# A fused attention, expert and mixer kernel: the front of the mixer reordered

## The chip, the cores and the metric

The kernel runs on one core of a Trainium2 chip. The metric is the device time of one execution, in microseconds. Before the change the median of three runs is 624.88 us (624.0 to 626.03). TensorE multiplies matrices, VectorE, ScalarE and GpSimd work on vectors, SyncE (SP) only starts transfers. In the rows they are PE (PEld for its weight loads), DVE, ACT, POOL and SP.

## The reference

Three layers follow each other, on 2 batches of 768 tokens with 384 values each. The first is a linear attention with a delta rule. The second sends every token to one of 8 experts. The third, the mixer, is the one that the change is mostly about:

```
def _moe2_ref(x, w_ch1, w_ch2):
    X = np.fft.fft(x, axis=1)
    X = np.fft.fft(X, axis=2)
    mixed = np.real(X).astype(np.float32)
    u = x + mixed
    mu = np.mean(u, axis=-1, keepdims=True)
    var = np.mean((u - mu) ** 2, axis=-1, keepdims=True)
    un = (u - mu) / np.sqrt(var + 1e-06)
    ch = np.maximum(un @ w_ch1, 0.0) @ w_ch2
    return (u + ch).astype(np.float32)
```

`w_ch1` is 384 x 1536, `w_ch2` 1536 x 384. In the expert layer each token's chosen expert is the argmax of its gate logits, or the expert of the token before it where a local gate says so; its output is p[e] * (relu(x @ w1[e]) @ w2[e]).

## The kernel before

**Splits.** To keep float32 accuracy, every operand of a large product is split into a high part (rounded, by a ScalarE copy) and a low part (the difference, by VectorE or GpSimd). A product then takes three matmuls: high by high, low by high, high by low. For the weights these are `whi` (ScalarE) and `wlo` (VectorE, which then also issues the load of the weights six steps ahead on SP).

**Routing and experts.** `route` ranks the tokens of each expert on VectorE and TensorE and makes the lists for gathers and scatters. `moe_main` runs 32 steps of one quarter expert each: `h` (first product, relu and split), `whi` and `wlo` for later steps, `o` (second product). It starts with `chosen`, the low splits of three weight blocks, and the transposes of expert 0's tokens (`xtr`). Between the steps it decodes the mixer's weights, which arrive as 64-bit numbers (`decoding`, a generator that is advanced step by step). The last step ends with two scatters of token rows to `x2d` in HBM, issued by GpSimd. Behind them stand 24 warm-up products (`WARMM`) and the splits of the last three weight blocks, 35 to 37.

**The mixer** reads `x2d` again. The sequence of 768 is treated as 6 x 128. `load` brings x of one batch in three transfers (pairs of row blocks, i = 1, 2, 0), then `ur`, the same rows in output order, on SP; two of its six tiles are gathered by GpSimd. `sums` (even half) and `difs` (odd half) combine the blocks; `split` splits the results (`zh`, `zl`). `along` does one residue k2: products along the sequence (`yp`), their split (`evac`), products along the features (`fp`), then the two output tiles m that mirror each other, each added to its tile of `ur` (`add`). `stats` takes mean and variance and normalises (`un`), `untr` transposes and splits the result (`uT`). `mlp1` and `mlp2` then run over 12 tiles in `GROUPS=(2,4,4,2)`; the tiles of a batch come in the order 2, 4, 1, 5, 0, 3, so group 0 is the two tiles of k2 = 2 of the first batch. `warm` runs products on the first part of x to keep TensorE busy.

**The order of the work** in the mixer is not written out. Each step is a generator that yields costs (engine, ns), flags to wait for and resources to take or return. `Order` simulates them once, when the program is built, and emits instructions in the order in which its engines would grant them. Priorities are in `MP` (lower goes first), `EB` holds a bias for VectorE in the choice between VectorE and GpSimd (`tt`, `eng`); it is a bias on the planned cost. What comes out is a fixed order on each engine; every engine works in order.

Of the kernel before, what the change touches and what calls it, by code (L numbers as in the profile page):

```python
# [6 lines left out]
F32 = mybir.dt.float32  # L7
# [722 lines left out]
class Rest:  # L730
# [4 lines left out]
    def route(s,keep,pool,ps,lg):  # L735
# [54 lines left out]
        s.Wr=T("W",[128,4,2,12,8],F16); s.ph=T("ph",[128,4,2,12],F16); pp=s.pp=pool.tile([128,4,12],F16,name="pp")  # L790
# [8 lines left out]
        V.tensor_copy(out=pp[:,0],in_=tok)  # L799
        s.parts(0)  # L800
# [139 lines left out]
    def moe_main(s):  # L940
        dec=s.decoding(); s.sc=[]; s.scattered=[]; last=None
        s.chosen()
        s.wlo(0); s.wlo(1)
        for k in range(3): s.xtr(0,k,"h",3)
        s.wlo(2)
        next(dec)
        for q in range(32):
# [6 lines left out]
            last=x  # L954
            s.wlo(q+3)
# [19 lines left out]
    WARMM=24  # L975
# [102 lines left out]
    def load(s,b):  # L1078
# [27 lines left out]
    def tt(s,out,a,b,op,x):  # L1106
        e,c=s.eng(469,956,s.EB.get(x,0))
        yield c
        e.tensor_tensor(out=out,in0=a,in1=b,op=op)  # L1109
    def stt(s,out,a,x,b):  # L1110
        yield ("V",469)
        s.nc.vector.scalar_tensor_tensor(out=out,in0=a,scalar=x,in1=b,op0=ALU.mult,op1=ALU.add)
    def buf(s,n,b): return s.fq.tile([128,384],F32,tag=n,name=n,bufs=1)
    def sums(s,b):
# [53 lines left out]
    def split(s,b,k,z):  # L1168
        yield ("+","z")
        h=s.fq.tile([128,384],F32R,tag="zh",name="zh",bufs=4); l=s.fq.tile([128,384],F32R,tag="zl",name="zl",bufs=4)  # L1170
        yield ("A",413)
# [6 lines left out]
    EB={'q1': -500, 'q0': 0, 'D1': -2000, 'z0': -500, 'S0': -2000, 'S1': 1000, 'z1': 1000, 'D0': 500}  # L1178
    WARM,PHASE=18,0
    MP={'M1': 0, 'M2': 2.48, 'R': 0, 'F': 0.26, 'a02': 1.67, 'a01': 2.48, 'a00': 0, 'a03': 0.58, 'a12': 1.4, 'a11': 0.19, 'a10': 2.06, 'a13': 1.84, 'L1': 1.44, 'u11': 2.35, 'q00': 1.26, 'z02r': 1.07, 'z11r': 1.2, 'e10': 0.65, 'D1': 1.9, 'q01': 2.35, 'u14': 0.69, 'q03': 0.52, 'q11': 1.03, 'e12': 2.33, 'S1': 0.4, 'z02i': 1.72, 'D0': 1.75, 'u13': 0.39, 'q02': 1.0, 'q05': 2.0, 'z01i': 0.51, 'u00': 0.67, 'u02': 0.79, 'e02': 1.68, 'z12r': 0.29, 'q14': 2.09, 'e01': 2.48, 'e11': 2.42, 'e00': 1.31, 'q15': 2.4, 'u03': 1.82, 'u15': 1.94, 'e03': 1.49, 'u10': 1.32, 'z12i': 1.87, 'z11i': 1.57, 'z01r': 1.37, 'u12': 2.13, 'u01': 1.05, 'e13': 1.85, 'q13': 0.71, 'q04': 2.47, 'q12': 0.26, 'q10': 0.16, 'u05': 1.84, 'S0': 0.76, 'u04': 1.14}  # L1180
    def along(s,b,k2):

        nc,o=s.nc,s.o; V=nc.vector
        ks=[("0",0)] if k2==0 else [("3",3)] if k2==3 else [(f"{k2}r",k2),(f"{k2}i",3+k2)]
        for n,_ in ks: yield f"z{b}{n}"
        yield ("+","Y")
        Y=[s.fq.tile([128,3,256],F32R,tag=f"Y{i}",name="Y",bufs=2) for i in range(2)]
        for d in range(3):
            yield ("+","h")
            p=s.ps.tile([128,256],F32,tag="h",name="yp",bufs=3)  # L1190
            yield ("T",330*len(ks),0) if d<2 else ("T",330*len(ks))
            n=0
            for z,t in ks:
                for a,c in ((0,0),(1,0),(0,1)):
                    nc.tensor.matmul(out=p,lhsT=s.z[b,z][a][:,128*d:128*d+128],rhs=s.seq[c][t],start=(n==0),stop=(n==3*len(ks)-1)); n+=1  # L1195
            s.add_(f"e{b}{k2}",s.evac(b,k2,d,p,Y,330*len(ks)))
# [4 lines left out]
        for d in range(3):  # L1201
            yield f"Y{b}{k2}{d}"
            yield ("T",620)
            for x in range(2):
                for a,c in ((0,0),(1,0),(0,1)):
# [4 lines left out]
        yield ("A",213)  # L1210
# [3 lines left out]
        for k,o1,o2 in kk:  # L1214
            yield ("+","m")
            m=s.fq.tile([128,384],F32,tag="m",name="m",bufs=1)
            yield ("V",540)
# [6 lines left out]
        for k in ks: yield f"u{b}{k}"  # L1224
        yield from s.stats(b,ks)
    def evac(s,b,k2,d,p,Y,t):
        yield ("",t+200)
        yield ("A",264)
        s.nc.scalar.activation(out=Y[0][:,d],in_=p,func=AF.Copy)
        yield ("V",335)  # L1230
# [8 lines left out]
    def stats(s,b,ks):  # L1239
        nc,o=s.nc,s.o; V=nc.vector; n=len(ks)  # L1240
        yield ("+","st")
        T=lambda nm,sh: s.fp.tile([128]+sh,F32,tag=nm,name=nm,bufs=2)
        ag=T("ag",[2,2]); v=T("vs",[4,2])
        for i,k in enumerate(ks):
            st=T(f"bs{i}",[6])
            yield ("V",469)
            V.bn_stats(out=st,in_=s.ur[b][:,k])
            yield ("V",75)
            V.bn_aggr(out=ag[:,i],in_=st)
        m,va=ag[:,0:n,0],ag[:,0:n,1]  # L1250
        v0,sd,r,nm=[v[:,i,0:n] for i in range(4)]
        yield ("V",75)
        V.tensor_scalar(out=v0,in0=va,scalar1=1e-6,scalar2=None,op0=ALU.add)
        yield ("A",95)
        nc.scalar.activation(out=sd,in_=v0,func=AF.Sqrt)
        yield ("V",80)
        V.reciprocal(out=r,in_=sd)
        yield ("V",75)
        V.tensor_tensor(out=r,in0=r,in1=v0,op=ALU.mult)
        yield ("V",75)  # L1260
        V.tensor_tensor(out=r,in0=r,in1=sd,op=ALU.add)
        yield ("V",75)
        V.tensor_scalar(out=r,in0=r,scalar1=0.5,scalar2=None,op0=ALU.mult)
        yield ("V",80)
        V.reciprocal(out=r,in_=r)
# [38 lines left out]
    def warm(s):  # L1304
# [9 lines left out]
        if s.WARM: yield from s.left_xa(0)  # L1314
    def w_ch1(s,x,k,f): return s.W[32+f//2][:,x,f%2,128*k:128*k+128]
# [167 lines left out]
```

## Time and profile before

The profiled execution took 627.96 us, its span is 626.2 us, with a mean granted TensorE clock of 0.905.

| engine | busy us | share of the span | instructions |
|---|---|---|---|
| PE (matmul) | 507.9 | 81% | 4986 |
| DVE | 421.7 | 67% | 950 |
| ACT | 323.7 | 52% | 745 |
| POOL | 88.1 | 14% | 89 |

Attention fills the span up to about 250 us, routing follows until 269 us, the experts until 410 us, and the mixer runs from there to the end. The shares are means over these stages, so they tell little of one stage; the rows below are of single stretches. In a row of the timeline, times are us from the span's start, then the busy time, the engine, the line of the kernel, the operation, what is written and read, the count, and in brackets the idle time before it with what ended it. In a row of the chain of waits stand the start, the length and the work that the end waited for. Two clock levels occur: 1.00 is 2.4 GHz, 0.50 is 1.2 GHz.

### The profile page before, as it was taken

How to read it: one execution, taken by the hardware profiler on the slowest of the kernel's cores; microseconds unless marked ns; L12 is line 12 of the kernel's file. 1: busy time of each engine (PE TensorE's matmuls, PEld its weight loads, DVE VectorE, ACT ScalarE, POOL GpSimd, SP SyncE). 2: the span in 40 equal slices, each digit the busy share in tenths (PEclk: the TensorE clock that was granted, in tenths of full speed). 3: DMA queues.
4: the chain of work that ended last, by engine and by line, in shares of the span. 5: the costliest groups of instructions: out<-in, count | busy, mean ns of one | idle time of the engine just before them, and what ended most of it. 6: DMA issues, size and time to landing. Idle time of an engine off the chain costs nothing.

```text
span 626.2 us, 12592 instructions
## 1 busy us (share of the span) xinstructions
PE 507.9 (81%) x4986; PEld 482.3 (77%) x4986; DVE 421.7 (67%) x950; ACT 323.7 (52%) x745; POOL 88.1 (14%) x89
## 2 busy tenths in 40 slices
PE   0333047894888999599999999978899999999997
PEld 0233037784778898589999999977799998998997
DVE  7968997868997963687788788767886731221122
ACT  3465177877788897346665656543454321111111
POOL 5000000000000000223212232243640000000010
PEclk9955558877989999599999999989699999999999
DMA  6722230341331525699789795235000000010010
GB/s 231 143 59 77 67 62 8 113 93 51 77 70 28 95 49 165 197 312 349 263 286 326 274 304 187 93 133 188 1 1 1 14 13 1 2 50 1 1 50 26
DMA packets 71438, 69.85 MB, mean 112 GB/s; under 512 B 44286, under 2 KB 63523, under 8 KB 71376
## 3 DMA queue, kind: packets, MB, share of 16 engines
q1 hardware_dynamic: 68240, 59.16, 31.8%
q0 software_dynamic: 3136, 9.85, 4.6%
q8 instruction: 40, 0.66, 0.4%
q14 instruction: 22, 0.18, 0.1%
HBM read 53.53 MB, written 7.86 MB: 98 GB/s over the span
## 4 chain that ended last, share of the span: by engine, by line
PE 38%; issue 13%; POOL 3%; DVE 2%; DMA 1%; ACT 1%; POOLq 0%; SPq 0%; ACTq 0%
PE mp L1330 12%; PE mop L1356 12%; PE hp L916 5%; PE op L927 4%; PE fp L1206 2%; PE yp L1195 1%; POOL xg L898 1%; POOL x2d L936 1%; PE up L1288 1%; POOL ur L1098 1%; DMA x2d<-ot,sim 1%; DMA xa<-x2d 0%; POOL e L1109 0%; POOL tab L1074 0%; PE xtp L904 0%
## 5 line engine op out<-in xcount | busy, mean ns | idle before, releaser
L1340 DVE SCALAR_TENSOR_TENSOR ml<-mp,mh 128x256 fp32r<-128x256 f32 (+1 forms) x48 | 26.8, 558 | 98.5 <-ACT mh L1338 98.3
L1330 PE MATMUL mp<-uT,ws 128*128 128x256 f32 (+1 forms) x432 | 85.3, 343 | 0.2 <-DVE ml L1340 0.2
L1338 ACT ACTIVATE mh<-mp 128x256 fp32r<-128x256 f32 (+1 forms) x48 | 23.6, 491 | 115.7 <-PE mp L1330 115.7
L1356 PE MATMUL mop<-ws,mh 128*128 128x384 f32 x288 | 81.6, 338 | 0.0
L1330 PEld LDWEIGHTS mp<-uT,ws 128*128 128x128 f32 x432 | 69.5, 193 | 9.0 <-DVE ml L1340 0.8
L916 PE MATMUL hp<-xT,ws 128*128 128x256 f32 x576 | 74.0, 283 | 1.1 <-DVE xT L907 1.1
L916 PEld LDWEIGHTS hp<-xT,ws 128*128 128x128 f32 x576 | 72.5, 190 | 1.3 <-DVE xT L907 1.3
L927 PE MATMUL op<-ws,hh 128*128 128x384 f32 x256 | 72.1, 343 | 0.0
L309 PEld LDWEIGHTS <-KT 128*128 128x128 f16 x576 | 25.9, 113 | 58.7 <-issue 31.0
L309 PE MATMUL ga<-ST,KT 128*128 128x64 f16 x288 | 16.4, 227 | 57.0 <-DVE ST L305 50.6
L891 DVE TENSOR_TENSOR ws<-raw,ws 128x1536 fp32r<-128x1536 f32 x32 | 56.0, 1751 | 0.0
L1356 PEld LDWEIGHTS mop<-ws,mh 128*128 128x128 f32 x288 | 52.8, 188 | 0.8
L888 ACT ACTIVATE ws<-raw 128x1536 fp32r<-128x1536 f32 x32 | 47.4, 1487 | 2.6 <-DMA raw<-moe_w 2.6
L1356 PE MATMUL mop<-ws,ml 128*128 128x384 f32 x144 | 48.3, 335 | 0.0
L927 PEld LDWEIGHTS op<-ws,hh 128*128 128x128 f32 x256 | 46.8, 188 | 0.0
L927 PE MATMUL op<-ws,hl 128*128 128x384 f32 x128 | 42.9, 335 | 0.0
L919 DVE SCALAR_TENSOR_TENSOR hl<-hp,hh 128x512 fp32r<-128x512 f32 x32 | 22.1, 691 | 27.4 <-ACT hh L918 27.3
L898 POOL DMA_INDIRECT xg<-xd,gm x16 | 21.7, 1356 | 120.4 <-DMA raw<-moe_w 113.7
L918 ACT ACTIVATE hh<-hp 128x512 fp32r<-128x512 f32 x32 | 19.0, 593 | 36.0 <-PE hp L916 36.0
L936 POOL DMA_INDIRECT x2d<-ot,sim x16 | 21.5, 1347 | 101.6 <-ACT ot L932 99.2
L368 DVE TENSOR_TENSOR tmp<-Gu,P 128x31 f32<-128x31 f32 (+15 forms) x93 | 31.5, 339 | 1.9
L370 DVE TENSOR_TENSOR P<-P,tmp 128x31 f32<-128x31 f32 (+15 forms) x93 | 31.4, 337 | 1.7
(268 smaller groups left out, 1224.1 us busy)
## 6 DMA issues: line engine op xcount, KB each, us to landing
raw<-moe_w SPq DMA_DIRECT2D x64, 384.0 KB, 5.5
x<-moe_w_ch SPq DMA_DIRECT2D x24, 384.0 KB, 6.3
qp<-q SPq DMA_DIRECT2D x6, 512.0 KB, 3.9
kp<-k SPq DMA_DIRECT2D x6, 384.0 KB, 4.7
vp<-v SPq DMA_DIRECT2D x6, 384.0 KB, 5.2
xd<-yb SPq DMA_DIRECT2D x48, 48.0 KB, 1.7
xa<-x2d SPq DMA_DIRECT2D x6, 384.0 KB, 4.0
tab<-seq POOLq DMA_DIRECT2D x2, 768.0 KB, 7.2
```

Of the source, the lines that this page charges most:

```text
L309: s.nc.tensor.matmul(out=out,lhsT=st[l],rhs=mv[m],start=(first and i==0),stop=True,skip_group_check=True)
L368: nc.vector.tensor_tensor(out=x,in0=Gu[:,k,k+1:32].unsqueeze(2).to_broadcast([128,m,n]),in1=P[:,k,0:n].unsqueeze(1).to_broadcast([128,m,n] ...
L370: nc.vector.tensor_tensor(out=P[:,k+1:32,0:n],in0=P[:,k+1:32,0:n],in1=x,op=ALU.subtract)
L888: s.nc.scalar.activation(out=s.W[q][:,0].rearrange("p s c -> p (s c)"),in_=s.raw[q],func=AF.Copy)
L891: s.nc.vector.tensor_tensor(out=W[1],in0=s.raw[q],in1=W[0],op=ALU.subtract)
L898: nc.gpsimd.indirect_dma_start(out=s.xg[e][t],out_offset=None,in_=s.xd,in_offset=bass.IndirectOffsetOnAxis(ap=s.gi[:,8*t+e:8*t+e+1],axis=0))
L916: nc.tensor.matmul(out=p[:,i],lhsT=s.W[q][:,a,i,128*k:128*k+128],rhs=xT[b][:,k],start=(n==0),stop=(n==8)); n+=1
L927: nc.tensor.matmul(out=s.po[t],lhsT=hs[a][:,i,128*t:128*t+128],rhs=s.W[q][:,b,i,384:768],start=(g==0 and i==0 and n==0),stop=(g==3 and i== ...
L936: i=s.nc.gpsimd.indirect_dma_start(out=s.x2d,out_offset=bass.IndirectOffsetOnAxis(ap=s.si[:,c:c+1],axis=0),in_=ot,in_offset=None,bounds_ch ...
L1330: nc.tensor.matmul(out=p,lhsT=s.w_ch1(a,k,f),rhs=s.uT[g][b][:,k,0:N],start=(n==0),stop=(n==8)); n+=1
L1340: nc.vector.scalar_tensor_tensor(out=hl,in0=p,scalar=0.0,in1=hh,op0=ALU.max,op1=ALU.subtract)
L1356: nc.tensor.matmul(out=pm[t],lhsT=hs[a][:,128*t:128*t+128],rhs=s.w_ch2(b,f),start=(f==0 and n==0),stop=(f==11 and n==2))
```

## The change

- `route`: the token number is copied right after the one-hot of the expert is made; its product with that one-hot (`Wt`) stands behind the rank products, and one product each with the two rank halves takes the place of `parts(0)`.
- `moe_main`: the low split of weight block 1 goes behind the transposes, that of block 2 into the first step. At the end GpSimd sets a word to zero (queued behind the scatters), VectorE copies it, and only then come the low split of block 35 and the splits of 36 and 37. The warm-up is 38 products.
- `load`: `ur` is loaded once the third part of x has landed. ScalarE writes one column of it from x, which SP's transfer then waits for.
- `EB`: all sums and low splits of the first batch go to VectorE (-9000). `sums` makes the difference of parts 1 and 2, and starts its split, ahead of the third part. Planned costs and `MP` are new throughout, `WARM` is 16 instead of 18.
- `along`, first batch, k2 = 2: the products of the imaginary part run first, into all three banks, those of the real part follow, and each of the two tiles gets its own `stats`. The order of the three matmuls of a product is high-high, high-low table, low-high.
- `stats`: ScalarE takes half the standard deviation straight from the variance (scale 0.25, bias 0.25e-6), one reciprocal, two fused VectorE operations and one more reciprocal give the refined 1/sd: two VectorE operations less.
- `fill`: four 128-column products on a unit matrix at a time, with the lowest priority and a pause of 500 ns in the plan, from the imaginary part's split until group 0 is complete. They hold one of the four `o` banks.
- `mlp1`: the three kinds of matmul are the outer loop and the three blocks of k the inner one.

```diff
@@ route
+        pp=s.pp=pool.tile([128,4,12],F16,name="pp"); pp0=pp[:,0]
         V.tensor_tensor(out=Ot,in0=it,in1=b3(e),op=ALU.is_equal)
+        V.tensor_copy(out=pp0,in_=tok)
+        Wt=T("Wt",[128,12,8],F16)
...
+        V.tensor_tensor(out=Wt,in0=Ot,in1=b3(pp0),op=ALU.mult)
...
-        V.tensor_copy(out=pp[:,0],in_=tok)
-        s.parts(0)
+        for h in range(2): V.tensor_tensor(out=s.Wr[:,0,h],in0=Wt,in1=b3(s.hi[:,h]),op=ALU.mult)
@@ moe_main
-        s.wlo(0); s.wlo(1)
+        s.wlo(0)
         for k in range(3): s.xtr(0,k,"h",3)
-        s.wlo(2)
+        s.wlo(1)
...
+            if q==0: s.wlo(2)
             s.wlo(q+3)
...
+        z=s.wk.tile([128,2],F32,name="z")
+        s.nc.gpsimd.memset(z[:,0:1],0.0)
+        s.nc.vector.tensor_copy(out=z[:,1:2],in_=z[:,0:1])
+        for _ in dec: pass
         s.wlo(35)
-        for _ in dec: pass
         for q in (36,37):
             s.whi(q); s.wlo(q)
-    WARMM=24
+    WARMM=38
@@ load
+        yield f"xa{b}0"
+        yield ("A",150)
+        nc.scalar.activation(out=ur[:,0,0:1],in_=xa[0][:,0:1],func=AF.Copy)
         yield ("Q",475)
         nc.sync.dma_start(out=ur[:,0:4],in_=w[:,0:4])
-        yield f"xa{b}0"
@@ sums
         yield from s.tt(t[3],t[1],t[2],A,f"S{b}")
+        yield from s.tt(t[1],t[1],t[2],S,f"S{b}")
+        s.add_(f"z{b}2i",s.split(b,"2i",t[1]))
         yield f"xa{b}0"
         yield from s.tt(t[0],x[0],x[3],A,f"S{b}")
         yield from s.left_xa(b)
-        yield from s.tt(t[1],t[1],t[2],S,f"S{b}")
-        s.add_(f"z{b}2i",s.split(b,"2i",t[1]))
@@ class
-    EB={'q1': -500, 'q0': 0, 'D1': -2000, 'z0': -500, 'S0': -2000, 'S1': 1000, 'z1': 1000, 'D0': 500}
-    WARM,PHASE=18,0
+    EB={'q1': 500, 'q0': -9000, 'D1': 0, 'z0': -9000, 'S0': -9000, 'S1': -500, 'z1': 1000, 'D0': -9000}
+    WARM,PHASE=16,0
@@ along
+        early=b==0 and k2==2
+        def product(d,zs,first,last):
+            for z,t in zs:
+                for a,c in ((0,0),(0,1),(1,0)):
+                    nc.tensor.matmul(out=p[d],lhsT=s.z[b,z][a][:,128*d:128*d+128],rhs=s.seq[c][t],start=first,stop=last and z==zs[-1][0] and a==1); first=False
+        p={}
+        if early:
+            yield f"z{b}2i"
+            for d in range(3):
+                yield ("+","h")
+                p[d]=s.ps.tile([128,256],F32,tag="h",name="yp",bufs=3)
+                yield ("T",375,0)
+                product(d,ks[1:],True,False)
+            ks=ks[:1]
...
-        for k in ks: yield f"u{b}{k}"
-        yield from s.stats(b,ks)
+        if early:
+            for k in ks: s.add_(f"u{b}{k}",s.stats(b,[k]))
+        else: yield from s.stats(b,ks)
@@ stats
-        V.tensor_scalar(out=v0,in0=va,scalar1=1e-6,scalar2=None,op0=ALU.add)
-        nc.scalar.activation(out=sd,in_=v0,func=AF.Sqrt)
+        nc.scalar.activation(out=h,in_=va,func=AF.Sqrt,scale=0.25,bias=s.eps)
...
+        V.scalar_tensor_tensor(out=w,in0=va,scalar=1e-6,in1=r,op0=ALU.add,op1=ALU.mult)
+        V.scalar_tensor_tensor(out=w,in0=w,scalar=0.25,in1=h,op0=ALU.mult,op1=ALU.add)
@@ fill (new, called in mixer behind warm)
+        yield "z02i"
+        yield ("+","o")
+        p=s.ps.tile([128,512],F32,tag="o",name="wq",bufs=4)
+        while "n01" not in s.o.flags and s.o.now<100000:
+            yield ("T",220)
+            for _ in range(4): s.nc.tensor.matmul(out=p[:,0:128],lhsT=s.K["identh"],rhs=s.K["identh"],start=True,stop=True)
+            yield ("",s.FILL)
+        yield ("-","o")
@@ mlp1
-                for k in range(3):
-                    for a,b in ((0,0),(1,0),(0,1)):
-                        nc.tensor.matmul(out=p,lhsT=s.w_ch1(a,k,f),rhs=s.uT[g][b][:,k,0:N],start=(n==0),stop=(n==8)); n+=1
+                for a,b in ((0,0),(1,0),(0,1)):
+                    for k in range(3): nc.tensor.matmul(out=p,lhsT=s.w_ch1(a,k,f),rhs=s.uT[g][b][:,k,0:N],start=(n==0),stop=(n==8)); n+=1
```

## Rows read from the trace of the kernel before

**Rows 1.** Windows: stretch, length, busy (count) of PE, PEld, DVE, ACT, POOL, clock, DMA
```profile
435.00:438.80 3.80, 2.28 (x19) 1.94 (x17) 3.20 (x14) 1.45 (x4) 0.64 (x1) 1.00 0.02 8
438.80:444.70 5.90, 4.06 (x15) 3.11 (x16) 4.91 (x10) 3.23 (x8) 5.62 (x6) 0.50 0.01 3
444.70:449.00 4.30, 4.30 (x20) 4.30 (x21) 3.85 (x7) 0.77 (x2) 2.26 (x3) 0.50 0.00 0
449.00:480.00 31.00, 30.56 (x233) 29.16 (x233) 24.49 (x76) 15.64 (x41) 9.93 (x9) 1.00 0.00 1
```

**Rows 2.** Chain of waits: start us, us, what
```profile
409.96 2.44 POOL x2d L936
...
412.71 3.46 DMA x2d<-ot,sim
...
416.29 3.09 DMA xa<-x2d
...
444.70 2.29 PE mp L1330 x9
...
619.26 2.62 PE mop L1356 x15
```

**Rows 3.** Timeline, routing and first expert: start, us, engine, line, operation [idle before]
```profile
256.95 0.17 DVE L813 TENSOR_TENSOR ph<-pp,hi 128x24 f16<-128x24 f16 x1
...
269.13 4.57 PE L916 MATMUL hp<-xT,ws 128*128 128x256 f32 x36 [1.08 <-DVE xT L907]
```

**Rows 4.** Timeline around the scatters, VectorE and GpSimd
```profile
378.91 1.15 POOL L936 DMA_INDIRECT x2d<-ot,sim  x1 [11.36 <-ACT ot L932]
...
409.75 1.75 DVE L891 TENSOR_TENSOR ws<-dec,ws 128x1536 fp32r<-128x1536 f32 x1
...
412.12 3.43 DVE L891 TENSOR_TENSOR ws<-dec,ws 128x1536 fp32r<-128x1536 f32 x2 [0.62 <-ACT ws L888]
...
412.71 2.06 POOL L936 DMA_INDIRECT x2d<-ot,sim  x1 [0.30 <-issue]
```

**Rows 5.** Timeline, VectorE's first sums
```profile
419.40 0.56 DVE L1109 TENSOR_TENSOR d<-xa 128x384 f32<-128x384 f32 x1 [3.85 <-DMA xa<-x2d]
...
423.72 0.57 DVE L1109 TENSOR_TENSOR e<-xa 128x384 f32<-128x384 f32 x1 [1.22 <-DMA xa<-x2d]
...
424.21 0.55 DVE L1109 TENSOR_TENSOR d<-xa 128x384 f32<-128x384 f32 x1
```

**Rows 6.** Line 1094, the load of ur: both transfers, issue to landing
```profile
DMA to landing us min/median/max: 7.5/8.3/9.1
```

**Rows 7.** Chain of waits: products along the sequence and features at full clock
```profile
461.36 0.65 PE fp L1206 x6
...
472.97 1.07 PE yp L1195 x9
```

**Rows 8.** Timeline, TensorE: the first feature products
```profile
429.81 2.26 PE L1206 MATMUL fp<-tab,Y 128*128 128x194 f32 x18 [0.39 <-DVE Y L1231]
```

**Rows 9.** Statistics by tile and timeline, up to the first MLP product
```profile
L1247 DVE BATCH_NORM_STATS2 bs<-ur x12: 526/551/561, 434.8 to 501.2; 128x6 f32<-128x384 f32 x12
...
434.63 1.01 POOL L1109 TENSOR_TENSOR ur<-ur,m 128x384 f32<-128x384 f32 x1 [2.93 <-DVE m L1219]
...
441.08 0.87 PE L1288 MATMUL up<-ca,un 128*128 128x128 f32 x3 [1.26 <-ACT un L1272]
...
442.50 1.35 DVE L1109 TENSOR_TENSOR zl<-e,zh 128x384 fp32r<-128x384 f32 x1
```

**Rows 10.** Windows of lines 1195 and 1206 alone: PE, PEld, clock, DMA
```profile
419.40:444.70 25.30, 8.14 (x45) 6.75 (x45) 0.77 0.46 164
...
419.40:444.70 25.30, 4.65 (x36) 4.25 (x36) 0.77 0.46 164
```

**Rows 11.** Timeline, group 1: its last tile's split, its first product
```profile
480.15 0.55 DVE L1295 TENSOR_TENSOR uT<-up,uT 128x384 fp32r<-128x384 f32 x1
...
490.95 2.26 PE L1330 MATMUL mp<-uT,ws 128*128 128x512 f32 x9
```

More of the change, by code (lines that the diff above doesn't have):

```diff
@@ L789, in route @@
         hi=s.hi=T("hi",[128,2,12],F16); lo=T("lo",[128,12],F16)
-        s.Wr=T("W",[128,4,2,12,8],F16); s.ph=T("ph",[128,4,2,12],F16); pp=s.pp=pool.tile([128,4,12],F16,name="pp")
+        s.Wr=T("W",[128,4,2,12,8],F16); s.ph=T("ph",[128,4,2,12],F16)
         oh=s.oh=pool.tile([128,12,128],F16,name="oh")
@@ L1106, in tt @@
     def tt(s,out,a,b,op,x):
-        e,c=s.eng(469,956,s.EB.get(x,0))
+        e,c=s.eng(550,1270,s.EB.get(x,0))
         yield c
@@ L1110, in stt @@
     def stt(s,out,a,x,b):
-        yield ("V",469)
+        yield ("V",550)
         s.nc.vector.scalar_tensor_tensor(out=out,in0=a,scalar=x,in1=b,op0=ALU.mult,op1=ALU.add)
@@ L1188, in along @@
         for d in range(3):
[L1189 to L1196, printed above, removed]
+            if not early:
+                yield ("+","h")
+                p[d]=s.ps.tile([128,256],F32,tag="h",name="yp",bufs=3)
+            yield ("T",375*len(ks),0) if d<2 else ("T",375*len(ks))
+            product(d,ks,not early,True)
+            s.add_(f"e{b}{k2}",s.evac(b,k2,d,p[d],Y,375*len(ks)))
+        if early: yield ("-","z")
         for _ in ks: yield ("-","z")
@@ L1202, in along @@
             yield f"Y{b}{k2}{d}"
-            yield ("T",620)
+            yield ("T",690)
             for x in range(2):
-                for a,c in ((0,0),(1,0),(0,1)):
+                for a,c in ((0,0),(0,1),(1,0)):
                     nc.tensor.matmul(out=p[:,x],lhsT=Y[a][:,d,128*x:128*x+128],rhs=s.fea[c][d][:,x],start=(n==0),stop=True,skip_group_check=True); n+=1
@@ L1209, in along @@
         q=s.fq.tile([128,194],F32,tag="q",name="q",bufs=1)
-        yield ("A",213)
+        yield ("A",335)
         nc.scalar.activation(out=q,in_=p[:,1],func=AF.Copy)
@@ L1216, in along @@
             m=s.fq.tile([128,384],F32,tag="m",name="m",bufs=1)
-            yield ("V",540)
+            yield ("V",650)
             V.tensor_tensor(out=m[:,0:193],in0=p[:,0,0:193],in1=q[:,0:193],op=o1)
@@ L1240, in stats @@
         nc,o=s.nc,s.o; V=nc.vector; n=len(ks)
+        for k in ks: yield f"u{b}{k}"
         yield ("+","st")
@@ L1245, in stats @@
             st=T(f"bs{i}",[6])
-            yield ("V",469)
+            yield ("V",550)
             V.bn_stats(out=st,in_=s.ur[b][:,k])
-            yield ("V",75)
+            yield ("V",150)
             V.bn_aggr(out=ag[:,i],in_=st)
         m,va=ag[:,0:n,0],ag[:,0:n,1]
-        v0,sd,r,nm=[v[:,i,0:n] for i in range(4)]
-        yield ("V",75)
-        V.tensor_scalar(out=v0,in0=va,scalar1=1e-6,scalar2=None,op0=ALU.add)
-        yield ("A",95)
-        nc.scalar.activation(out=sd,in_=v0,func=AF.Sqrt)
[L1256 to L1265, printed above, removed]
-        yield ("V",75)
+        h,r,w,nm=[v[:,i,0:n] for i in range(4)]
+        yield ("A",200)
+        nc.scalar.activation(out=h,in_=va,func=AF.Sqrt,scale=0.25,bias=s.eps)
+        yield ("V",150)
+        V.reciprocal(out=r,in_=h)
+        yield ("V",150)
+        V.scalar_tensor_tensor(out=w,in0=va,scalar=1e-6,in1=r,op0=ALU.add,op1=ALU.mult)
+        yield ("V",150)
+        V.scalar_tensor_tensor(out=w,in0=w,scalar=0.25,in1=h,op0=ALU.mult,op1=ALU.add)
+        yield ("V",150)
+        V.reciprocal(out=r,in_=w)
+        yield ("V",150)
         V.scalar_tensor_tensor(out=nm,in0=m,scalar=-1.0,in1=r,op0=ALU.mult,op1=ALU.mult)
@@ L1286, in untr @@
         p=s.ps.tile([128,3,128],F32,tag="t",name="up",bufs=1)
-        yield ("T",330)
+        yield ("T",255)
         for j in range(3): nc.tensor.transpose(p[:,j],un[:,128*j:128*j+128],s.K["ident"])
@@ L1291, in untr @@
         c=slice(128*i,128*i+128)
-        yield ("A",371)
+        yield ("A",490)
         nc.scalar.activation(out=uh[:,:,c],in_=p,func=AF.Copy)
-        yield ("V",469)
+        yield ("V",540)
         V.tensor_tensor(out=ul[:,:,c],in0=p,in1=uh[:,:,c],op=ALU.subtract)
@@ L1314, in warm, with fill @@
         if s.WARM: yield from s.left_xa(0)
+    def fill(s):
+        yield "z02i"
[6 more added lines that the diff above has]
+        yield ("-","o")
+    FILL=500
     def w_ch1(s,x,k,f): return s.W[32+f//2][:,x,f%2,128*k:128*k+128]
@@ L1320, in mlp1 @@
             N=128*m
-            for i in range(m): yield f"n{g}{i}"
             for f in range(12):
+                if f==0:
+                    for i in range(m): yield f"n{g}{i}"
                 yield ("+","mh")
@@ L1334, in relu @@
         nc=s.nc
-        yield ("",1930*m/4+200)
+        yield ("",2090*m/4+200)
         hh,hl=[s.fq.tile([128,512],F32R,tag=n,name=n,bufs=3)[:,0:128*m] for n in ("mh","ml")]
@@ L1353, in mlp2 @@
                 for t in range(m):
-                    if t==0 or f==11: yield ("T",483*m if f<11 else 483,0)
+                    if t==0 or f==11: yield ("T",530*m if f<11 else 530,0)
                     for n,(a,b) in enumerate(((0,0),(1,0),(0,1))):
@@ L1376, in mixer @@
         s.ur={}; s.uT={}; s.z={}; s.xa={}; s.nxa={}; s.hs={}; s.nfin={}
-        sq=s.fp.tile([128,1],F32,name="sq")
+        sq=s.fp.tile([128,1],F32,name="sq"); s.eps=s.fp.tile([128,1],F32,name="eps")
+        s.nc.vector.memset(s.eps,0.25e-6)
         s.nc.vector.memset(sq,1.0)
@@ L1381, in mixer @@
         s.add_("W",s.warm())
+        s.add_("W",s.fill())
         for b in range(2):
```

12 lines of the change are left out of this document (6 added, 6 removed).

## The prediction

> **What bounds the kernel now.** I read the busy time by stretches first, because the stages have different limits. From 449 to 480 us TensorE is busy 30.56 of 31 us at granted clock 1.00, its level of 2.4 GHz [rows 1]. So once the MLP runs, the end is the moment at which TensorE has worked off its list. The chain of waits, read second, says where that begins: the first MLP product starts at 444.70, the last ones end at 619.26 + 2.62 = 621.88 [rows 2]. Ahead of 444.70 the chain is not TensorE's: a scatter from 409.96, the next with its transfer from 412.71, the load of x from 416.29 [rows 2], then sums, splits and statistics. TensorE had too little to do there: 2.28 of 3.8 us from 435.0 to 438.8; then the clock fell to 0.50 (1.2 GHz) until 449.0, with 4.06 of 5.9 us busy up to 444.7 [rows 1]. So the sum is: with the first MLP product s us earlier, w us of transform work not yet done by then, h us no longer lost to the half clock and f us of new losses, the end comes s - w + h - f earlier.
>
> **The change part by part**, in the times of the trace of before.
>
> Routing: the token copy and the product with the rank halves leave the chain, two small VectorE operations like the one of 0.17 us at 256.95 [rows 3], some 0.2 each. Their replacements stand where VectorE waits for the rank products. Bounds 0 (the gathers behind may wait for something else) and 0.4; I take 0.3.
>
> Start of the experts: the first product, at 269.13, had waited 1.08 for VectorE's split of xT [rows 3], behind two weight splits. With one ahead of it the copy of xT on ScalarE comes last, and the second weight split ends about when the second slice's product wants it. Bounds 0 and 1.1; I take 0.4. SP is touched too: two weight loads are issued behind the moved splits, one of them now behind six loads of the MLP's weights. They are for slices that are wanted four steps later, so I cost that at nothing; without this cover it is a late weight and a stall of some us. Together the experts end 0.7 us earlier.
>
> Scatters: VectorE's next three splits now wait for a memset that GpSimd reaches only behind both scatters. Queued behind that wait are the splits, and then the first sums; nobody else wants the three splits before the MLP. The two scatters took 2.44 and 2.06 us beside splits that ran from 409.75 and 412.12; one with no split beside it took 1.15 [rows 2, 4]. New: 409.96 + 1.15 + 0.30 + 1.15 = 412.56, landing 1.40 later as before (412.71 + 3.46 less 414.77), x's loads issued at 414.1 instead of 416.29. The handover by memset and copy is not in the trace: between 0.1 and 1.0 (a small VectorE operation, a GpSimd sum of 1.01, rows 9), I take 0.3. The splits then run from 412.9 to 418.1 (1.75 + 3.43, rows 4), so the first sum starts at 418.3 instead of 419.40 [rows 5]: half of the 2.2 is eaten by VectorE's own backlog. The Trainium skill (SBUF — State Buffer, "Who interferes with whom") says that a VectorE operation with two SBUF inputs blocks only GpSimd's reads, and infers that the writing of DMA descriptors is not hindered by it. By that rule the scatters stay as long and the wait only costs; the 2.44 beside a split against 1.15 without speaks against it.
>
> First sums: VectorE idled 1.22 until x's third part came at 423.72, and t0 followed at 424.21 [rows 5]; the load of ur, 768 KB, flew beside. Now ur is issued only once that part has landed. Issued 2.2 earlier and alone, the part lands between 417.2 (the first part's 3.09 of rows 2) and 421.5 (the old 7.4 from the first issue); I take 419.7. VectorE then goes from sum to sum, five of 0.56 [rows 5], and t0 starts at 421.1, 3.1 earlier; at the upper bound 2.7. ur lands 7.5 to 9.1 after its issue [rows 6], that is at 427.9 to 429.5 from 420.4; it is wanted 1.1 behind the feature products, at 429.1. ScalarE gets a small copy that waits for x; behind it stands a split whose sum ends later than that. I cost both at nothing, 0.4 at most.
>
> First transform by parts: 9 of its 18 products run before the second operand is there; 9 take 1.07 [rows 7], so what is left behind the last split is 1.0 shorter. Together 4.1: the feature products, from 429.81 to 432.07 [rows 8], end at 428.0.
>
> From there to the first MLP product it was 444.70 - 432.07 = 12.6. Off this go: the second tile's statistics ahead of the first's normalising, 0.55 [rows 9] and a small step of 0.2; two steps fewer, 0.4; two sets of transposes at full instead of half clock, 0.87 each before [rows 9], so 0.87 together; a split of 1.35 beside GpSimd, against 0.56 alone [rows 5, 9]: 0.8; the second tile's sum on VectorE instead of 1.01 on GpSimd [rows 9]: 0.45. That is 3.3, which leaves 9.3: first MLP product at 437.3, and 0.7 earlier with the experts, 436.6. s = 8.1. Bounds: 4.8 (the 12.6 stays, since VectorE has the odd half's sums to do as well) and 10.
>
> w: before 444.70 TensorE had done 45 products along the sequence and 36 along features [rows 10]. By 436.6 I expect 36 and 18: 9 x 0.119 + 18 x 0.108 = 3.0 are left for later [rows 7]. Bounds 1 and 5.
>
> h: 444.7 to 449.0 ran fully busy at clock 0.50 [rows 1]: 2.2 come back if the clock stays, which the longer warm-up (38 products for 24) and the fillers are for. Bounds 0 and 2.2; I take 2.2.
>
> f: a filler pack has 4 x 128 columns, as many as two products along the sequence, so 0.24 [rows 7]. TensorE takes its work in order, and each of some eight handovers on the chain can be late by a pack: 0 to 3.5 with other waits; I take 1.8.
>
> Sum: 8.1 - 3.0 + 2.2 - 1.8 = 5.5 us. The profiled execution (span 626.2, 627.96 in all) is 3.1 above the median of 624.88; the gain lies in fixed stretches, so I take it off the median: **619.4 us**. The list behind keeps TensorE fed: group 1's last tile is split at 480.15 and its first product starts at 490.95 [rows 11]; 5.5 earlier leaves 4.7 even if that tile gains nothing.
>
> **Rivals.** The clock falls all the same. For it: it fell at 438.8 though TensorE had been busy 2.28 of the 3.8 us before [rows 1], so sparse fillers may not do. Against: the real products lie closer now. Then h is 0 and the transposes stay at half clock: 5.5 - 2.2 - 0.9 = 2.4, 622.5. The Trainium skill (TensorE: Matmul & The Clock Gate, "What's actually happening") lets the clock fall after idleness; here it fell behind a stretch that was not idle.
>
> The scatters stay long. For it only the inference quoted; against it the rows. The memset comes at 415.0, the first sum at 420.4, all behind it 2.1 later than forecast: 621.5.
>
> The front moves little. VectorE alone has all sums, splits, evacuations and statistics of the first batch; if the new priorities put other tiles' work between, the first product comes at 441, and 3.7 - 3.0 + 2.2 - 1.8 = 1.1: 623.8, no change that can be told. Against: two thirds of s lie ahead of the statistics.
>
> TensorE runs dry between groups 0 and 1: slower. For it: VectorE takes over the first batch's operations from GpSimd, and tile 3 of the first batch is the last that group 1 needs. If it ends later than 485.4 (490.95 - 5.5), TensorE waits, and a gap like that before 438.8 also brings the half clock for 10.2 us as from 438.8 to 449.0, 5.1 lost. With the tile at 489: 3.6 + 5.1 - 5.5 = 3.2 slower, 628.1. It decides from 485.9 on, where gap and clock together take the gain. Against: the tile is ready at 480.70 now, and most of what it waits for comes earlier.
>
> Better than forecast: w at 1, f at 0.3: 9.0, 615.9.
>
> **How the numbers follow.** Forecast 0.52 (its own range 616.5 to 622), better 0.08, clock 0.14, long scatters 0.07, front moves little 0.11, dry 0.08. A measurement of this kernel tells about 0.3% from no change, so same is 623.0 to 626.8. The first two are faster, and 0.17 of the next two: 0.77. Same 0.04 + 0.11 = 0.15, slower 0.08. The range goes from 615.0, under the better case, to 624.6, over the one in which the front moves little; out are the dry case and tails.
>
> **What would show it.** Scatters of 1.15 us; the first sum at about 417.6; x's third part there before VectorE wants it; clock 1.00 from the scatters to the end; the first MLP product at 436 to 437 and no idle TensorE from there. It is wrong if that product is later than 440, if the clock falls before it, or if TensorE has gaps between the groups.

## The result and the profile after

The changed kernel took 614.45 us (median of 4 runs, 614.05 to 616.09), the kernel before 625.36 beside it (624.0 to 626.03): a ratio of 0.9833, interval 0.9808 to 0.9859, 10.9 us faster where 5.5 were forecast. The forecast of 619.4 was 5 us too high, and the time lies 0.55 under the range of 615.0 to 624.6. On two other chips the changed kernel took 616.21 (ratio 0.9836, 0.98 to 0.9871) and 616.65 (0.9868, 0.9824 to 0.9913).

The profiled execution took 616.09 us, its span is 614.3. Its last product ends at 610.00, 11.88 earlier than before [rows 2]. 2.25 of that stand ahead of all changed code: attention ended that much earlier, and in the traces of this study, all with the same attention, its end lies anywhere between 246 and 251.5 us. So I compare stretches, not times from the span's start:

| stretch | before | after | gained |
|---|---|---|---|
| routing's first maximum to the first expert product | 18.86 | 18.09 | 0.77 |
| from there to the first of the last two scatters | 140.83 | 139.79 | 1.04 |
| from there to the first MLP product | 34.74 | 31.98 | 2.76 |
| from there to the end of the last product | 177.18 | 172.12 | 5.06 |

These gains add up to 9.63 us. The times on the two other chips differ by 9.65 and 9.36; of the 10.9 here the rest is less than what attention's end moves.

The windows of the kernel after (columns as in [rows 1]), the first two up to the first sum and the first feature product, the last one over all that follows the first MLP product:

```profile
405.80:414.40 8.60, 8.60 (x78) 8.53 (x76) 5.17 (x6) 4.81 (x5) 4.45 (x4) 1.00 0.31 103
414.40:421.50 7.10, 6.87 (x57) 6.13 (x56) 6.30 (x13) 2.21 (x6) 3.38 (x4) 1.00 0.87 273
421.50:437.88 16.38, 14.87 (x144) 13.72 (x144) 14.55 (x42) 7.01 (x19) 2.26 (x2) 1.00 0.39 135
437.88:610.00 172.12, 172.12 (x1048) 162.16 (x1047) 67.30 (x170) 46.07 (x103) 18.88 (x18) 1.00 0.04 12
```

The same view of the kernel before, over all behind its first MLP product:

```profile
444.70:621.88 177.18, 176.74 (x1064) 165.32 (x1065) 70.57 (x184) 45.07 (x103) 17.09 (x17) 0.99 0.03 12
```

The clock column is 1.00 throughout, where [rows 1] had 0.50, and TensorE has no idle time left behind the first MLP product. Its count there is 1048 instead of 1064: less work is left.

How long the clock is at half differs between executions of the kernel before. f3_tile, a run told of below, has the mixer of the kernel before. There it was at 0.50 from 437.2 to 440.7 only, and up again ahead of the first MLP product:

```profile
440.75:616.48 175.73, 174.76 (x1065) 163.30 (x1065) 70.57 (x184) 45.18 (x103) 18.13 (x18) 1.00 0.03 12
```

From the scatters to that product it took 33.58 us, to the end 209.31; the profiled execution of before took 34.74 and 211.92. So up to 2.6 us of the gain in the table above may be how the clock fell in that one execution.

The chain of waits of the kernel after, which answers to [rows 2, 5, 7]:

```profile
405.90 0.82 POOL x2d L939
...
407.23 3.98 DMA x2d<-ot,sim
411.35 3.06 DMA xa<-x2d
414.43 0.56 DVE d L1120
...
417.87 0.48 DVE zl L1120
418.40 1.10 PE yp L1200 x7
...
422.75 5.71 DMA xa<-x2d
428.56 0.20 ACT ur L1104
...
430.57 0.72 ACT un L1296
...
437.34 0.71 PE fp L1231 x6
438.05 3.36 PE mp L1365 x27
...
607.38 2.62 PE mop L1391 x15
```

Up to 418.40 this is the chain forecast. Then TensorE itself stands in it, fillers and warm-ups among its work, and from 422.75 a load that the forecast did not have on the path: x of the second batch, for which ScalarE's small copy waits at 428.56, ahead of the first tile's square root. The chain ends in feature products of the next transform (437.34), ahead of the first MLP product in TensorE's order.

### The profile page after: what moved, and what is told of

Read it like the earlier page. It is cut to its first block, busy times and chain, and to the rows that moved or that the text cites. A ratio compares the mean times of both kernels' runs of the same rounds, so it can differ in the third digit from the quotient of the medians.

```text
span 614.3 us, 12751 instructions
## 1 busy us (share of the span) xinstructions
PE 504.7 (82%) x5070; PEld 480.6 (78%) x5070; DVE 419.5 (68%) x946; ACT 325.3 (53%) x748; POOL 81.9 (13%) x85
## 4 chain that ended last, share of the span: by engine, by line
PE 39%; issue 11%; DMA 2%; POOL 2%; DVE 1%; ACT 0%; POOLq 0%; ACTq 0%; SPq 0%
PE mp L1365 12%; PE mop L1391 12%; PE hp L919 5%; PE op L930 4%; PE fp L1231 2%; PE yp L1200 2%; DMA xa<-x2d 1%; POOL xg L901 1%; PE up L1312 1%; DMA x2d<-ot,sim 1%; POOL x2d L939 0%; DVE d L1120 0%; PE xtp L907 0%; POOL tab L1082 0%; DVE ur L1399 0%
## 5 line engine op out<-in xcount | busy, mean ns | idle before, releaser
L1365 PE MATMUL mp<-uT,ws 128*128 128x256 f32 (+1 forms) x432 | 82.8, 337 | 0.0
L939 POOL DMA_INDIRECT x2d<-ot,sim x16 | 19.1, 1191 | 99.1 <-ACT ot L935 96.6
```

The lines of the kernel that those rows point to most:

```text
L1365: for k in range(3): nc.tensor.matmul(out=p,lhsT=s.w_ch1(a,k,f),rhs=s.uT[g][b][:,k,0:N],start=(n==0),stop=(n==8)); n+=1
```

## The experiments

Two theories stood against each other. By the first, the gain is a matter of supply: what counts is how much transform work TensorE has done by the first MLP product. By the second, the gain is the clock and the shorter chain to that product. The four runs of the first group had one edit each of the changed kernel, on one chip (its kernel before: 627.33); the control ran on the next.

**Fillers (e1_nofill), the wait behind the scatters (e2_nowait), the warm-up (e3_warm24), the late load of ur (e4_ur_first).**

```diff
@@ e1_nofill: fill, its pauses and its plan kept
-            for _ in range(4): s.nc.tensor.matmul(out=p[:,0:128],lhsT=s.K["identh"],rhs=s.K["identh"],start=True,stop=True)
@@ e2_nowait: moe_main
-        z=s.wk.tile([128,2],F32,name="z")
-        s.nc.gpsimd.memset(z[:,0:1],0.0)
-        s.nc.vector.tensor_copy(out=z[:,1:2],in_=z[:,0:1])
@@ e3_warm24
-    WARMM=38
+    WARMM=24
@@ e4_ur_first: load
-        nc.scalar.activation(out=ur[:,0,0:1],in_=xa[0][:,0:1],func=AF.Copy)
```

> The changed kernel without the filler products; their place in the plan stays, so every other instruction keeps its order. Theory clock (most of the gain comes from a clock that stays at 1.00 from the scatters to the end): the clock falls to 0.50 between 425 and 438 us, the time is 2 to 5 us above the changed kernel's 614.45. Theory supply (the gain comes from VectorE, which feeds TensorE earlier, and the fillers only fill): the clock stays or its fall costs little, 614 to 615, perhaps 0.5 less since no product waits behind a filler.

> The changed kernel with the memset and copy taken out, so the last three splits run beside the scatters again. If the wait works as its rows suggest: scatters of 2.0 to 2.4 us instead of 1.0, x's load issued about 0.9 later, 615.2 to 616. Rival (transfers, not descriptors, set the landing): no difference, 614.3 to 614.7, because the landing came 2.97 after the end of the second scatter's issue with the wait and 1.40 without.

> The changed kernel with 24 instead of 38 warm-up products behind the experts. Theory clock: TensorE idles about 3 us before x lands, the clock falls there and stays at 0.50 for some 7 us or more, the first transforms run at half clock, 1 to 3 us more than 614.45. Theory supply: the first transforms wait for VectorE anyway, 614 to 615.

> The changed kernel without ScalarE's small copies, so ur is loaded right behind x and ScalarE waits for no x. If ur beside x delays x's third part as in the kernel before: VectorE idles some 1 to 2 us ahead of t0, 615.5 to 616.5. Rival (what the copy keeps ScalarE waiting, 1.4 us at 428.5, costs as much as it saves): 613.5 to 615.

> The changed kernel itself, as the mark for the others of this call on the same chip. From the first scatter to the end of the last product 204.1 us in its trace, as before. In the trace of the kernel without fillers the clock fell for one stretch of 3.4 us only, and in four traces of the first call the stretch from the first MLP product to the end was 172.1 us each time.

Measured: 617.03, 617.0, 614.34 and 617.6 us; the control, the changed kernel itself, 616.21 on its chip. As ratios 0.9851 (0.9808 to 0.9894), 0.9874 (0.9826 to 0.9922), 0.9823 (0.9779 to 0.9868), 0.9867 (0.9826 to 0.9909), control 0.9836: none of them can be told from it. From the scatters to the end the traces have 204.41, 204.37, 203.26 and 205.27, controls 203.82 and 204.76.

Without the fillers the clock does fall, as these windows of e1_nofill show:

```profile
420.20:424.90 4.70, 3.38 (x28) 3.01 (x27) 4.08 (x9) 1.49 (x4) 1.84 (x2) 1.00 0.88 298
424.90:428.30 3.40, 3.40 (x18) 3.31 (x17) 2.74 (x8) 0.93 (x4) 0.45 (x1) 0.50 0.38 90
```

Behind 3.38 of 4.70 us busy it went to 0.50 for 3.4 us. But it was back before the first MLP product, and the stretch to the end, 204.41, lies between those of the controls: where TensorE waits for others, half a clock cost little here. In the same stretch with fillers it stays at 1.00, with 38 warm-up products or 24; in e3 TensorE stood idle for 2.99 us in one piece ahead of the first x, and the clock stayed too. The Trainium skill (TensorE: Matmul & The Clock Gate, "What's actually happening") ties the lower clock to idleness; here, as in [rows 1], it followed a stretch that was mostly busy.

The scatters of e2_nowait, GpSimd's timeline, and those of the kernel after:

```profile
404.02 2.44 POOL L939 DMA_INDIRECT x2d<-ot,sim  x1 [9.71 <-ACT ot L935]
406.76 2.07 POOL L939 DMA_INDIRECT x2d<-ot,sim  x1 [0.30 <-issue]
```

```profile
405.90 1.03 POOL L939 DMA_INDIRECT x2d<-ot,sim  x1 [9.71 <-ACT ot L935]
407.23 1.01 POOL L939 DMA_INDIRECT x2d<-ot,sim  x1 [0.30 <-issue]
```

The wait alone makes them short, so it was the splits that stretched them: the inference of the Trainium skill that the forecast weighed (SBUF — State Buffer, "Who interferes with whom") does not hold here. But the 2.5 us saved bring the first sum only 1.0 nearer to the scatters (8.53 for 9.55), and nothing at the end.

In e4_ur_first ur and x share the queues again, and VectorE waits for x's third part, as in [rows 5]:

```profile
418.09 0.56 DVE L1119 TENSOR_TENSOR d<-xa 128x384 f32<-128x384 f32 x1 [2.01 <-DMA xa<-x2d]
```

In the kernel after that sum follows without a wait, at 417.31, but in f5_control, the same kernel again, it waits as well:

```profile
417.38 0.56 DVE L1120 TENSOR_TENSOR d<-xa 128x384 f32<-128x384 f32 x1 [1.38 <-DMA xa<-x2d]
```

Of the fourteen traces with the late load two have a wait there (f5 and g2, 0.65), of the six with ur beside x all but e8. So the late load makes the wait rarer and does not end it. The first MLP product came 33.19 after the scatters in e4, 31.70 to 32.67 in the three traces of the changed kernel.

**One part alone on the kernel before, and VectorE's part taken out of the changed one.** e6_experts_only has the edits of `moe_main`; e8_fill_only has `fill` and the 38 warm-up products; f1_vectore_only has the bias; e7_gpsimd is the changed kernel with the first batch's bias gone.

```diff
@@ f1_vectore_only: kernel before
-    EB={'q1': -500, 'q0': 0, 'D1': -2000, 'z0': -500, 'S0': -2000, 'S1': 1000, 'z1': 1000, 'D0': 500}
+    EB={'q1': -500, 'q0': -9000, 'D1': -2000, 'z0': -9000, 'S0': -9000, 'S1': 1000, 'z1': 1000, 'D0': -9000}
@@ e7_gpsimd: changed kernel
-    EB={'q1': 500, 'q0': -9000, 'D1': 0, 'z0': -9000, 'S0': -9000, 'S1': -500, 'z1': 1000, 'D0': -9000}
+    EB={'q1': 500, 'q0': 0, 'D1': 0, 'z0': -500, 'S0': -2000, 'S1': -500, 'z1': 1000, 'D0': 500}
```

> The kernel before with the changes of the expert stage alone: the two splits moved, memset and copy behind the scatters, 38 warm-up products. Routing and mixer as before. By the prediction's terms: 0.4 from the experts' start and 1.1 to 2.2 from the scatters, 623 to 624 where the kernel before is 625.4. If scatters set little (the call before: 0.3 us with and without the wait): 624.5 to 625.4. The expert stage, first product to first scatter, took 140.83 before and 139.79 in every changed kernel: 139.79 here too if the moved splits or the added tile do it, 140.83 if it is the routing's new tile.

> The kernel before with the fillers and the 38 warm-up products alone. Theory clock: the clock stays at 1.00 from the scatters on, the 10.2 us at half clock before 449 go, 3 to 6 us less than the kernel before. Theory supply: it stays, but VectorE is as late as before; 0 to 2.5 us less, since the first MLP product moves by less than 1.5 us.

> The changed kernel with the old bias for the first batch (S0 -2000, D0 500, z0 -500, q0 0), so that GpSimd gets some of its sums again; the plan is made anew. Theory supply: VectorE and GpSimd slow each other and the tiles of the first batch come later; the first MLP product 2 us or more later, fewer transforms done ahead of it, 617 to 619. Theory clock: nothing that the clock sees changes, within 1 us of the changed kernel.

> The kernel before, with nothing changed but the bias that puts all sums and low splits of the first batch on VectorE. Theory supply (TensorE's list, not the chain to the first MLP product, was what ran short, and GpSimd's slow share of the sums was why): from the first MLP product to the end it takes some 173 us instead of 177.2, the whole 2 to 5 us less than before. Rival, the clock and the new plan carry the gain and the bias needs both: under 1.5 us less, and the stretch behind the first MLP product stays at 175 or more.

> The changed kernel as it is, the mark for the others on this chip: some 10 us less than the kernel before, from the scatters to the end 203.8 to 204.1 us, clock 1.00 from the scatters to the end.

| run | us | ratio to before | scatters to first MLP product | from there to the end |
|---|---|---|---|---|
| e6_experts_only | 624.4 | 0.999 (0.9959 to 1.0022) | 32.85 | 175.69 |
| e8_fill_only | 625.0 | 0.9989 (0.9956 to 1.0021) | 33.20 | 175.72 |
| f1_vectore_only | 629.63 | 1.0077 (1.0047 to 1.0107) | 36.52 | 178.99 |
| e7_gpsimd | 622.61 | 0.9943 (0.9918 to 0.9968) | 34.55 | 173.77 |
| f5_control | 616.65 | 0.9868 (0.9824 to 0.9913) | 32.67 | 172.09 |

The first two are no change that can be told, though both keep more of the clock (1.00 all through in e8). The interval of e8 still leaves the clock up to 2.75 us; its trace, 208.92 from the scatters to the end, is only 0.4 shorter than that of f3_tile. f1 missed its expectation on the wrong side: VectorE alone on the old plan is slower by 3.6 us (the medians) to 4.8 (the ratio), while taking it out of the changed kernel costs 6.4: 622.61, where 617 to 619 were expected. Part of these 6.4 can be the clock's, which in e7 was at 0.50 from 436.7 to 440.1, ahead of the first MLP product. In f1 VectorE has more to do up to the first MLP product (busy 25.48 us for 24.66) and waits longer for x (6.6 for 5.5). Its timeline:

```profile
423.74 0.56 DVE L1109 TENSOR_TENSOR d<-xa 128x384 f32<-128x384 f32 x1 [2.75 <-DMA xa<-x2d]
```

and its window behind the first MLP product, with 2.24 us of idle TensorE and 176.75 of work:

```profile
445.44:624.43 178.99, 176.75 (x1065) 166.12 (x1064) 71.24 (x189) 44.86 (x103) 12.62 (x12) 0.98 0.03 12
```

So the bias gained nothing without the changed plan and the earlier x; which of the two it needs was not taken apart.

**Transform by parts, statistics by tile, the second batch's copy.** f2_whole and f4_one_copy change the kernel after as the diff says, each alone; g1_whole_one_copy has both, since f2 lost time to another wait too (ScalarE's copy stood 2.44 us ahead of a split). g2_parts_joint and g3_whole_tile have f4's edit and one of the two halves of f2's each, g4_copy_warm f4's edit and 24 warm-up products; g5_mark is f4 again.

```diff
@@ load: f4_one_copy, and all g runs
-        nc.scalar.activation(out=ur[:,0,0:1],in_=xa[0][:,0:1],func=AF.Copy)
+        if not b: nc.scalar.activation(out=ur[:,0,0:1],in_=xa[0][:,0:1],func=AF.Copy)
@@ along: f2_whole, g1 (products and statistics), g3 (products only)
-        early=b==0 and k2==2
+        early=False
@@ along, the statistics' branch: g2 (joint)
-        if early:
+        if False:
@@ along, the statistics' branch: g3 (by tile)
-        if early:
+        if b==0 and k2==2:
```

> The changed kernel with the first transform whole (no imaginary part first) and the statistics of its two tiles together, order planned anew. Theory that the parts and the statistics by tile are on the path: the feature products end 0.5 to 1 us later, the first MLP product 1 to 3 us later, and the whole is 1 to 3 us above the control. Rival, TensorE's list bounds and fills the difference: the first MLP product comes later but what follows it is shorter by as much, and the whole is within 0.5 of the control.

> The changed kernel without ScalarE's small copy for the second batch (its load of ur then goes out at once). In the trace after, that copy waits 1.42 us for x of the second batch, with the first tile's square root queued behind it. Theory that this holds up the statistics: the first MLP product comes 0.7 to 1.4 us earlier, the whole 0.3 to 1 us below the control. Rival, the square root waits for VectorE's variance anyway, or TensorE has other work: within 0.3 of the control.

> The changed kernel with the first transform whole, the two tiles' statistics together, and ScalarE's small copy for the first batch only. In the run with the first transform whole (4.7 us more than its control from the scatters to the end) that copy waited 2.44 us for the second batch's x, ahead of a split that TensorE's odd half wanted. Theory that the parts are what counts: it stays 3 us or more above the control in that stretch (207 us or more) and 4 or more in the time. Rival, the copy's wait was the loss: the stretch comes to 205 to 206.5 us, and the time within 2.5 of the control.

> The changed kernel with the second batch's small copy gone and, in the first transform, the parts kept but the statistics of its two tiles together. Theory that the statistics tile by tile are what lets TensorE do the next transform while it waits: from the first MLP product to the end 175 to 176 us as with the whole transform, the time 3 to 5 us above the mark. Rival, the parts do it: 172 to 173 us there, within 1.5 of the mark.

> The changed kernel with the second batch's small copy gone and, in the first transform, the products whole but the statistics tile by tile. By the theory of the statistics: 172 to 173 us from the first MLP product to the end, the first transform product 1.5 us later after the scatters, the time 0.5 to 2 above the mark. By the rival, that the parts do it: 175 to 176 us, 3 to 5 above the mark.

> The changed kernel with two edits that each cost nothing or gained a little: no small copy for the second batch, and 24 warm-up products for 38. If both add, it is 0.3 to 1.2 us below the changed kernel (0.9815 to 0.985 of the kernel before); if they hide each other, equal to the mark within 0.4.

> The changed kernel with the second batch's small copy gone, the mark on this chip: 0.983 to 0.987 of the kernel before, 203.4 us from the scatters to the end, 172.1 of them behind the first MLP product.

| run | us | ratio to before | scatters to first MLP product | from there to the end |
|---|---|---|---|---|
| f2_whole (neither) | 622.72 | 0.9955 (0.9925 to 0.9984) | 32.67 | 176.10 |
| g1_whole_one_copy (neither) | 621.85 | 0.9952 (0.9923 to 0.998) | 31.11 | 176.16 |
| g2_parts_joint (parts) | 619.33 | 0.9902 (0.9864 to 0.9939) | 33.13 | 174.09 |
| g3_whole_tile (by tile) | 615.91 | 0.9864 (0.9817 to 0.9911) | 32.95 | 172.12 |
| f4_one_copy (both) | 615.95 | 0.9862 (0.9822 to 0.9902) | 31.32 | 172.08 |
| g5_mark (both, again) | 616.3 | 0.986 (0.9814 to 0.9906) | 31.91 | 172.09 |
| g4_copy_warm (both) | 615.55 | 0.9858 (0.9811 to 0.9905) | 30.95 | 172.10 |

This speaks for supply: the clock alone (e8) gave nothing that can be told, and an early MLP product alone is not enough either. f2 lost 6.1 us where 1 to 3 were expected. g1 met the numbers of its theory that the parts are what counts, but g2 and g3 put most of the loss on the statistics; g2's 174.09 behind the first MLP product, with 45 and 48 products done and 1.40 us of gaps, lies between the two values expected. In g1 the first MLP product comes as early as in the marks, and what follows takes 4.1 us more; with the statistics by tile, and only those, it is back at 172.12. g1's windows, behind the third block's feature products and behind the first MLP product:

```profile
433.47:439.48 6.01, 4.24 (x46) 3.58 (x43) 4.21 (x13) 3.64 (x8) 0.00 (x0) 1.00 0.00 0
439.48:615.64 176.16, 174.94 (x1066) 164.39 (x1067) 70.13 (x177) 47.26 (x104) 16.59 (x16) 1.00 0.04 12
```

and g3's behind its own:

```profile
440.00:612.12 172.12, 172.12 (x1047) 162.16 (x1046) 67.37 (x170) 46.08 (x103) 18.89 (x18) 1.00 0.04 12
```

2.82 us more work is left in g1 (174.94 for 172.12), 42 products along the sequence and 36 along features being done by then where g3 had 45 and 54, and 1.22 of gaps. TensorE's timeline of g1 shows what it did instead:

```profile
434.20 0.40 PE L1346 MATMUL wq<-ca 128*128 128x128 f16 x4
435.44 0.55 PE L1312 MATMUL up<-ca,un 128*128 128x128 f32 x3 [0.84 <-ACT un L1296]
435.82 0.83 PE L1346 MATMUL wq<-ca 128*128 128x128 f16 x12
437.25 0.52 PE L1312 MATMUL up<-ca,un 128*128 128x128 f32 x3 [0.59 <-ACT un L1296]
```

Between the two tiles' transposes stand only fillers; in the kernel after, real products stand there:

```profile
431.33 0.55 PE L1312 MATMUL up<-ca,un 128*128 128x128 f32 x3 [0.25 <-ACT un L1296]
...
433.08 0.48 PE L1200 MATMUL yp<-tab,zh 128*128 128x256 f32 x2
...
435.31 0.81 PE L1231 MATMUL fp<-tab,Y 128*128 128x194 f32 x6
435.96 0.49 PE L1312 MATMUL up<-ca,un 128*128 128x128 f32 x3
```

f2, g1 and g2 keep the priorities, but their order is planned anew, so what they lose is the loss of that half and of its plan together. The parts as such are worth 1.1 to 1.7 us in the traces (205.07 in g3 against 203.40 and 204.00 from the scatters to the end, in f4 and g5), nothing in the times. The second batch's copy costs nothing that can be told either; g4, the fastest in its trace (203.05), is not told from the changed kernel. The loop order of `mlp1`, the shorter formula of `stats` and the new priorities were not taken alone; f2 and g1, which keep all three, have 174.9 us of work behind the first MLP product, e6 and e8, which have none of them, 174.7 to 174.8, so no work saved there shows.

**The expert stage.** It lost 1.04 us in every kernel that has the changed routing (139.78 to 139.80) and nothing in e6, e8 and f1 (140.84 to 140.88), though e6 has all of `moe_main`'s edits. What is left is routing's new tile, which moves what is set aside behind it. f3_tile adds that tile to the kernel before and never uses it.

```diff
@@ route: f3_tile, kernel before
+        Wt=T("Wt",[128,12,8],F16)
```

> The kernel before with routing's new tile (128 partitions x 192 bytes) set aside and never used, which moves the addresses of what is set aside later. Theory that the changed kernel's shorter expert stage is a matter of where in SBUF its operands lie: 139.8 us from the first expert product to the scatters. Rival, it comes of an instruction of the change (the moved splits, the routing's order): 140.83 as before.

The stage took 139.61 (the one run 622.59, beside 626.73 for the kernel before; the clock also fell for less of the mixer there, so that difference is not the tile's alone). The chain, one step's first products, in the kernel before:

```profile
302.96 2.15 PE hp L916 x18
305.11 2.08 PE op L927 x12
```

in f3_tile:

```profile
303.09 2.09 PE op L928 x12
305.18 2.12 PE hp L917 x18
```

Of the two forms only hp is shorter, by 0.03 in each of 32 steps; over the stage its busy time fell from 74.0 to 72.9, which is most of the 1.22 that the stage lost. That the unused tile does it is shown, and all that it changes is where later tiles lie; why that counts is open: no run moved one operand alone.

## Why the prediction was wrong, by its own steps

With attention's 2.25 set aside, the terms are:

| term | forecast | measured | from |
|---|---|---|---|
| s | 8.1 | 4.57 | 0.77 + 1.04 + 2.76 |
| w | 3.0 | -2.47 | work behind the first MLP product: 176.74 less the 2.15 that 4.30 us at half clock lost [rows 1], against 172.12 |
| h | 2.2 | 2.15 | clock 1.00 |
| f | 1.8 | -0.44 | idle TensorE there: 177.18 - 176.74, against none |
| s - w + h - f | 5.5 | 9.63 | |

**The step that failed is w**, with bounds of 1 to 5: that by a first MLP product 8 us earlier TensorE would have done 36 products along the sequence and 18 along the features. It had done 45 and 54. The step behind it, that the way from the feature products to the MLP shrinks from 12.6 to 9.3, failed with it: it grew to 13.6 (424.30 to 437.88). The two are one thing. Statistics by tile put the second tile's behind the first's on VectorE and ScalarE instead of beside them: its normalising starts 4.0 us after the first's (430.57, 434.58) where the forecast took 0.55 off. In between VectorE and ScalarE prepared the next transform, and TensorE did it. So s gave 3.5 less, below its bound of 4.8, and w 5.5 more; in the sum the two errors cancel in part. Of the 2.76 of s behind the scatters, 0.91 came by the first sum and 3.26 by the first feature product, 0.46 went in the feature products (2.72 for 2.26) and 0.95 on the way behind them, which was to gain 3.3. g1 is in kind what I had forecast for the tail: an earlier MLP with more left over. It is 3.3 us worse than g5 in the trace, 5.7 by the ratios. s and w were worked out apart, as if TensorE stood still while the statistics ran.

**f was mis-sized and, as counted in the table, had the wrong sign.** A delay by filler packs shows once: the first feature products end 9.42 behind the first sum without the fillers, 9.87 in the kernel after, which s holds already. At the first MLP product no delay is left: it comes 32.31 after the scatters without fillers, though at half clock for 3.4 us, and 31.70 to 32.67 with them. And the gaps of before went away.

**h fits this one trace of before and no more.** Its 4.30 us at half clock behind the first MLP product were not there in f3_tile, where w comes out much the same without h (174.76 - 172.12 = 2.64). I took h off the median of all executions, and no run shows that the median lost it: e8, where the clock stayed, gained 0.9 us by the medians, with no change inside its interval.

**Right in size:** the first sums and parts, from the first sum to the first feature product 7.15 for 10.41, 3.26 shorter where 3.0 was forecast (4.1 less the first sum's own 1.1); routing and the start of the experts, 0.77 against 0.7; scatters of 1.03 against 1.15; ur in time.

**Right in kind, wrong in size:** the scatters' way to x. The second one ended 2.5 nearer to the first one's start (2.34 behind it for 4.81), but x's load was issued only 0.88 nearer to it (5.45 for 6.33): the rows landed 2.97 behind the end of the issue (407.23 + 3.98 less 408.24), not 1.40 as in [rows 2]. So the first sum waited 0.86 us for x and not, as forecast, for VectorE's own splits. It came 0.9 nearer, and 1.1 was forecast; two errors met.

**Not foreseen:** the 1.04 of the expert stage, and ScalarE's wait of 1.42 us for the second batch's x, which I had cost at nothing for the first batch alone.

Of the four rivals that were worse three did not come true: the clock stayed, the scatters were short, and TensorE had no gap at group 1. The third, that the front moves little, was half right: the first MLP product came 4.6 us earlier, 440.1 in the times of before, nearer to its 441 than to the forecast of 436.6 and just past the 440 that was named as a sign of being wrong; but the price that it put on this, 623.8, was not paid. "Better than forecast" came nearest in time (615.9), with s at 8.1, and with w at 1 still 3.5 too high.

## What to carry to other kernels

Where one engine bounds all that follows, a wait on its way is worth what it can do meanwhile: count the work left at the milestone, not only when the milestone comes, and work out the two together. Statistics of two tiles in turn beat both at once here by 3 us, since the time in between fed the next transform. Taking the bias to the faster engine out of its plan cost some 6 us, and putting it into the old plan cost 3.6 or more: test such an edit inside the plan that it belongs to. And take what the clock costs from more than one trace: that of before is 2.6 us longer, from the scatters to the end, than another with the same mixer.

## What the runs showed of the hardware

- An unused tile of 192 bytes a partition made 18 products of 256 columns 2.12 us long instead of 2.15.
- A scatter issued by GpSimd took 2.44 and 2.07 us beside VectorE's splits, 1.03 and 1.01 without; but its rows landed 2.97 us behind the issue instead of 1.40, so less than half of the saving reached the load behind it.
- A VectorE split beside GpSimd's sums took 1.27 us instead of 0.56 (the split before it, at 423.03), as these rows of the kernel after show, VectorE's timeline and GpSimd's:

```profile
424.65 1.27 DVE L1120 TENSOR_TENSOR zl<-e,zh 128x384 fp32r<-128x384 f32 x1 [0.59 <-ACT zh L1183]
```

```profile
424.52 2.27 POOL L1120 TENSOR_TENSOR d<-xa 128x384 f32<-128x384 f32 x2 [5.83 <-DMA xa<-x2d]
```
